# Weight sums by adding transfers and ScalarE copies instead of VectorE, and half of a group's first projection by 20 block products

## The chip, the cores and the metric

The kernel runs on one core of a Trainium2 chip, in float32. The metric is device time in microseconds of one launch, the median of several runs. Everything below concerns that one core: its TensorE (PE), VectorE (DVE), ScalarE (ACT), GpSimd (POOL), the SyncE queue (SP) that begins most loads, and the DMA engines.

## The reference

A gated linear attention is followed by a two-layer projection with SiLU between. Cut to what matters:

```
for t in range(768):                       # 4 batches x 8 heads, head size 48
    state = alpha[t][:, None] * state + outer(k[t], v[t])
    y[t]  = q[t] @ state
x = y as (3072 tokens, 384)
h = x @ w_in            # 384 x 2048
g = h * sigmoid(h)
out = g @ w_out         # 2048 x 384
```

The weights come as 64-bit floats and are rounded to float32 on the chip.

## The kernel before, in words

**Chunks and steps.** The 3072 tokens are cut into 24 chunks of 128 tokens (`n` = 0 to 23; `n` = 4 x position + batch). One step of the main loop works on two neighbouring chunks: `scores(n)` (PE products of `kp` and `qp`, copied by ACT into the tile `decayed`, then masked by POOL, line 813), `values(n)` (PE, copied by ACT into `xt`, line 851), `states(n)`, and for the next chunk `products` and `quotient` (all DVE: transposes at line 696, scans at 722 and 752, multiplications at 737, 739 and 758). A step has four slots. After each slot `fill` issues pieces of the projection until their share of work is due, so the PE always has projection work between the attention's short pieces. From the moment the tiles of `late` exist (`settle`, after the weights are converted, during chunk 7), every PE instruction is kept in the program's order, and so are the DVE sums.

**Groups.** Four chunks make a group (`grp` 0 to 5; 512 tokens), in two halves `h` of 256 tokens. The 2048 columns of `w_in` are taken as two pairs (`pair` 0 and 1). `enter_plain(grp, h, pair)` computes h = x @ w_in for one half and one pair the direct way: four pieces of six matmuls with 256 columns each, then one SiLU on ACT (line 909). `enter(grp, pair)` does both halves of a pair at once by a fast matrix multiplication on blocks: 20 products (list `PRODUCTS`) instead of the 24 of the direct way, a product being two matmuls. For this it needs sums of blocks of x (`sums_x`, list `SUMS_X`, 11 DVE instructions for each group) and sums of blocks of `w_in` (`sums_w`, list `SUMS_W`, 23 for each pair, once in the kernel). Blocks 0 to 11 are in the tile `w_in`, and are overwritten; 12 to 19 are in the tile `wx`. Then come copies and additions of the 20 results: ACT copies (line 936) and 14 DVE instructions (line 944, and 587 through `combine`) for each pair, and four SiLUs of double width (line 941). Three PSUM banks turn in this.

**Output.** `leave(grp, h)` computes out = g @ w_out by a scheme of seven products of eight matmuls; each product is a piece. `subtract` (line 1033) and `side_by_side` (line 1019) are DVE sums of parts of g that it needs. The results go out by transfers that POOL begins (line 1045).

**Order around the change.** Groups 0 and 1 are computed by `enter_plain`, groups 2 to 5 by `enter`. The list `pieces` has: all of group 0's plain pieces; `enter_plain(1, 0, 0)`; `leave(0, 0)`; `enter_plain(1, 1, 0)`; then the seven pieces of `leave(0, 1)` alternating with the eight of `enter_plain(1, 0, 1)` and `enter_plain(1, 1, 1)`; then for group 2 and the later ones `sums_x(grp)`, and `leave(grp-1, 0)` alternating with `enter(grp, 0)`, `leave(grp-1, 1)` with `enter(grp, 1)`. The sums of `w_in` are issued four at a time at the end of each `leave` piece (`done`): those of pair 0 during `leave(0, 1)`, those of pair 1 during `leave(1, 0)`.

The kernel also audits its inputs with DVE reductions (line 685), which start later, and has a general path that these inputs do not take.

Of the kernel before, what the change touches and what calls it, by code (L numbers as in the profile page):

```python
# [13 lines left out]
ALU = mybir.AluOpType  # L14
# [337 lines left out]
)  # L352


@with_exitstack
def quotients(
    ctx: ExitStack,
# [19 lines left out]
    dve, act, gps = nc.vector, nc.scalar, nc.gpsimd  # L377
# [197 lines left out]
    def block_w(at):  # L575

        return quads[:, at // NKT, at % NKT] if at < 4 * NKT else late["wx"][:, at - 4 * NKT]


    def combine(to, sa, a, sb, b):  # L580
        if sa == sb == 1:
            return dve.tensor_tensor(to, a, b, ALU.add)
        if sa == 1:
            return dve.tensor_tensor(to, a, b, ALU.subtract)
        if sb == 1:
            return dve.tensor_tensor(to, b, a, ALU.subtract)  # L586
        return dve.scalar_tensor_tensor(to, a, -1.0, b, ALU.mult, ALU.subtract)

    def sums_w(pair, upto):

        r = slice(2 * pair, 2 * pair + 2)
        while sums_done[pair] < min(upto, len(SUMS_W)):
            to, sa, a, sb, b = SUMS_W[sums_done[pair]]
            tc.keep_in_program_order(
                combine(block_w(to)[:, r], sa, block_w(a)[:, r], sb, block_w(b)[:, r]))
            sums_done[pair] += 1

    sums_done = [0] * (NQ // 2)
# [298 lines left out]
    def enter_plain(grp, h, pair):  # L897

        if h == 0:
            g_tiles(grp, pair)  # L900
        xt = xts[2 * grp + h]
        for f in range(8 * pair, 8 * pair + 8, 2):
            ps = bank(f // 2 % 3).rearrange("p (e n) -> p e n", e=2)
            for e in range(2):
                for t in range(NKT):
                    pe.matmul(ps[:, e, :], lhsT=w_in[:, t, (f + e) * 128 : (f + e + 1) * 128],
                              rhs=xt[:, t, :], start=(t == 0), stop=(t == NKT - 1))
            q, i = divmod(f, 4)
            act.activation(gts[grp, h, pair][:, i : i + 2, q % 2, :], ps, AF.Silu)  # L909
            if grp == 1 and pair == h == 0:  # L910
                differences(f // 2)
                differences(4 + f // 2)
            if grp > 0 and f % 8 == 6:
                side_by_side(grp, h, pair)
            yield

    def enter(grp, pair):
        g_tiles(grp, pair)
        halves = [gts[grp, h, pair] for h in range(2)]

        s = [halves[o % 2][:, o // 2] for o in range(8)]
        todo = iter(PRODUCTS)

        def new(i):
            return bank(i).rearrange("p (e n) -> p e n", e=2)

        def add(ps, first=False):
            w, x = next(todo)
            for e in range(2):
                pe.matmul(ps[:, e], lhsT=block_w(w)[:, 2 * pair + e], rhs=block_x(grp, x),  # L930
                          start=(first and e == 0), stop=(e == 1), skip_group_check=True)

        def copy(ps, to=None):
            if to is None:
                to = late["part"].tile([128, 2, TB], F32, name="part")
            act.copy(to, ps)  # L936
            return to

        def silu(h, i):
            x = halves[h][:, i : i + 2]  # L940
            act.activation(x, x, AF.Silu)  # L941

        def tt(to, a, b, op=ALU.add):
            dve.tensor_tensor(to, a, b, op)  # L944

        a, b, c = [new(i) for i in range(3)]
        add(a, True)
        copy(a, s[6])
        add(b, True)
        copy(b, s[2])  # L950
        add(c, True)
        tt(s[6], s[6], copy(c), ALU.subtract)
        yield
        add(a)
        t = copy(a)
        add(b)
        copy(b, s[4])
        add(c)
        copy(c, s[7])
        tt(s[7], s[7], t, ALU.subtract)  # L960
        yield
        add(a)
        copy(a, s[5])
        add(b)
        copy(b, s[3])
        tt(s[5], s[5], s[3])
        add(c)
        copy(c, s[0])
        yield
        add(a)  # L970
        tt(s[4], a, s[4])
        b = new(1)
        add(b, True)
        add(b)
        copy(b, s[1])
        yield
        c = new(2)
        add(c, True)
        tt(s[2], s[2], copy(c), ALU.subtract)
        a = new(0)  # L980
        add(a, True)
        tt(s[6], a, s[6])
        silu(0, 2)
        add(b)
        tt(s[5], copy(b), s[5], ALU.subtract)
        yield
        add(c)
        tt(s[1], c, s[1])
        tt(s[3], s[1], s[3], ALU.subtract)
        a = new(0)  # L990
        add(a, True)
        tt(s[2], a, s[2])
        add(b)
        tt(s[7], b, s[7])
        silu(1, 2)
        yield
        add(c)
        combine(s[1], -1, s[1], -1, s[0])
        tt(s[0], c, s[0])
        silu(0, 0)  # L1000
        a = new(0)
        add(a, True)
        tt(s[3], a, s[3])
        silu(1, 0)
        turn.append(turn.pop(0))
        for h in range(2):
            side_by_side(grp, h, pair)
        yield
# [7 lines left out]
    def side_by_side(grp, h, pair):  # L1016

        x = cells(grp, h, pair, 1, 0)
        dve.tensor_tensor(x, x, cells(grp, h, pair, 1, 1), ALU.add)

    def leave(grp, h):


        def product(ps, m, k, w, first=False):
            for i in range(HF):
                q = i // 2
                x = gts[grp, h, q // 2][:, 2 * (i % 2) + k, q % 2, m * C : (m + 1) * C]
                pe.matmul(ps, lhsT=x, rhs=w[:, i], start=(first and i == 0), stop=(i == HF - 1),
                          skip_group_check=True)

        def subtract(to, x, y):
            for pair in range(NQ // 2):
                dve.tensor_tensor(cells(grp, h, pair, *to), cells(grp, h, pair, *x),  # L1033
                                  cells(grp, h, pair, *y), ALU.subtract)

        def store(m, c, x, y=None):
            ci, b = divmod(GB * grp + 2 * h + m, B)
            o = opool.tile([128, HO], F32, name="o")
            if y is None:
                act.copy(o, x)  # L1040
            else:
                dve.tensor_tensor(o, x, y, ALU.add)  # L1042
            r = b * S + ci * C

            (gps if grp < NG - 1 else nc.sync).dma_start(out[r : r + C, c * HO : (c + 1) * HO], o)  # L1045

        u1, u2, u3, u4 = [rpool.tile([128, HO], F32, name=f"u{j}") for j in range(4)]
        steps = iter(range(7))

        def done():  # L1050
            if 2 * grp + h in (1, 2):
                sums_w(2 * grp + h - 1, 4 * next(steps) + 4)

        def new(i):
            return out_bank(i, HO)

        a, b = new(0), new(1)
        product(a, 0, 0, b11, True)
        act.copy(u1, a)
        subtract((0, 0), (1, 0), (0, 0))  # L1060
        done()
        yield
        product(b, 1, 0, t1, True)
        act.copy(u4, b)  # L1064
        done()
        yield
        product(a, 0, 1, b21)
        store(0, 0, a)
        subtract((0, 1), (0, 1), (0, 0))
        done()  # L1070
        yield
        b = new(1)
        product(b, 0, 0, t2, True)
        dve.tensor_tensor(u2, b, u1, ALU.add)
        subtract((1, 0), (1, 1), (0, 0))
        dve.tensor_tensor(u2, u2, u4, ALU.add)
        done()
        yield
        a = new(0)
        product(a, 0, 1, b22, True)  # L1080
        store(0, 1, a, u2)
        done()
        yield
        product(b, 1, 0, b12)
        dve.tensor_tensor(u3, b, u1, ALU.add)
        store(1, 1, u3, u4)
        done()
        yield
        a = new(0)
        product(a, 1, 1, t4, True)  # L1090
        store(1, 0, a, u3)
        done()
        yield
# [13 lines left out]
    def plain(grp, h, pair):  # L1107
        return (enter_plain(grp, h, pair), 12, 2 * (2 * grp + h) + 2)

    def group(grp):  # L1110
        return [[(enter(grp, pair), 12, GB * grp + GB)] * 7 for pair in range(2)]

    def output(grp):
        return [[(leave(grp, h), 12, GB * grp + GB)] * 7 for h in range(2)]
# [9 lines left out]
    pieces += [plain(1, 0, 0)] * 4 + [(leave(0, 0), 12, GB)] * 7  # L1124
    phases = [len(pieces)]
    pieces += [plain(1, 1, 0)] * 4
    both([(leave(0, 1), 12, GB)] * 7, [plain(1, 0, 1)] * 4 + [plain(1, 1, 1)] * 4)
    phases.append(len(pieces))
    before = output(1)
    for grp in range(2, NG):  # L1130
# [10 lines left out]
    def go_on():  # L1141

        nonlocal done
        next(pieces[done][0], None)
        done += 1

    audits = audit()
    done, bridged = 0, 0
    STEPS = NT + 1
    SLOTS = 4  # L1150
# [148 lines left out]
```

## Time and profile before

| | |
|---|---|
| median of 3 runs | 561.39 us (560.58 to 561.42) |
| span of the profiled execution | 558.1 us; the page gives no other time for it, so 3.3 us of the median lie around the span |
| PE busy | 541.4 us, 97% of the span |
| DVE busy | 445.1 us, 80% |
| ACT busy | 208.4 us, 37% |
| POOL busy | 75.9 us, 14% |
| granted TensorE clock | 0.994 on average |
| 46 sums of `w_in` on DVE | about 0.42 us each, between 150.7 us and 229 us |

A row of a timeline gives the start of a group of like instructions in us from the start of the span, the time to the end of its last one, the engine, the source line, the operation with output and inputs, the number of instructions (one float32 matmul of the program is two records on the PE), and, in brackets, how long the engine had been idle before and what released it. Matmuls are pipelined, so the distance between the starts of two neighbouring PE rows is what the first one costs.

### The profile page before, as it was taken

How to read it: one execution, taken by the hardware profiler on the slowest of the kernel's cores; microseconds unless marked ns; L12 is line 12 of the kernel's file. 1: busy time of each engine (PE TensorE's matmuls, PEld its weight loads, DVE VectorE, ACT ScalarE, POOL GpSimd, SP SyncE). 2: the span in 40 equal slices, each digit the busy share in tenths (PEclk: the TensorE clock that was granted, in tenths of full speed). 3: DMA queues.
4: the chain of work that ended last, by engine and by line, in shares of the span. 5: the costliest groups of instructions: out<-in, count | busy, mean ns of one | idle time of the engine just before them, and what ended most of it. 6: DMA issues, size and time to landing. Idle time of an engine off the chain costs nothing. (4 is left out here: it accounts for less than half of the span.)

```text
span 558.1 us, 12640 instructions
## 1 busy us (share of the span) xinstructions
PE 541.4 (97%) x5026; PEld 488.8 (88%) x5026; DVE 445.1 (80%) x801; ACT 208.4 (37%) x466; POOL 75.9 (14%) x146
## 2 busy tenths in 40 slices
PE   5999999999999999999999999999999999999996
PEld 3788887998899898899999999988998999998996
DVE  5887889974999799997998986998894775857531
ACT  3456643223333243353353353353263341432200
POOL 4100010221211211021021021021121000001000
PEclk9799999999999999999999999999999999999999
DMA  9999861164445525355445654717712122333101
GB/s 218 255 276 177 232 189 40 38 164 108 126 131 136 142 62 134 88 145 157 129 109 142 194 141 115 198 22 179 180 48 84 53 99 95 111 109 106 38 25 32
DMA packets 99220, 70.13 MB, mean 126 GB/s; under 512 B 56272, under 2 KB 88656, under 8 KB 99152
## 3 DMA queue, kind: packets, MB, share of 16 engines
q1 hardware_dynamic: 97232, 65.30, 44.6%
q0 software_dynamic: 1920, 3.93, 2.0%
q8 instruction: 41, 0.67, 0.5%
q14 instruction: 27, 0.22, 0.1%
HBM read 61.34 MB, written 7.86 MB: 124 GB/s over the span
## 5 line engine op out<-in xcount | busy, mean ns | idle before, releaser
L388 PE MATMUL ps_o<-w_out,g 128*128 128x192 f32 x768 | 134.7, 329 | 1.1 <-DVE o L1042 0.9
L388 PEld LDWEIGHTS ps_o<-w_out,g 128*128 128x128 f32 x768 | 125.4, 190 | 5.1 <-DVE o L1042 2.3
L388 PE MATMUL ps_m<-xt,w_in 128*128 128x256 f32 x480 | 113.6, 383 | 1.5 <-ACT xt L851 1.1
L388 PEld LDWEIGHTS ps_m<-xt,w_in 128*128 128x128 f32 x480 | 89.1, 190 | 14.4 <-ACT xt L851 1.6
L388 PE MATMUL ps_o<-wt,g 128*128 128x192 f32 x576 | 99.7, 326 | 0.0
L388 PEld LDWEIGHTS ps_o<-wt,g 128*128 128x128 f32 x576 | 95.1, 190 | 1.6 <-issue 0.2
L388 PE MATMUL ps_m<-xc,w_in 128*128 128x256 f32 x288 | 70.7, 382 | 0.0
L685 DVE TENSOR_REDUCE seen<-bits 128x1 f32<-128x384 int32 (+2 forms) x65 | 42.5, 689 | 24.0 <-DMA bits<-in_moe_w_out_dram 19.6
L388 PEld LDWEIGHTS ps_m<-xc,w_in 128*128 128x128 f32 x288 | 53.6, 190 | 7.0 <-DVE g L944 0.3
L941 ACT ACTIVATE g<-g 128x1024 f32<-128x1024 f32 x32 | 33.0, 1056 | 59.0 <-DVE g L944 59.0
L1033 DVE TENSOR_TENSOR g<-g 128x512 f32<-128x512 f32 x72 | 49.8, 708 | 6.1 <-PE ps_o L388 6.1
L1045 POOL DMA_DIRECT2D out_dram<-o x40 | 22.0, 550 | 223.2 <-DVE o L1042 127.6
L813 POOL TENSOR_SCALAR_AFFINE_SELECT g<-g 64x256 f32<-64x256 f32 x64 | 34.2, 534 | 124.8 <-ACT g L806 105.8
L388 PE MATMUL ps_m<-xc,wx 128*128 128x256 f32 x192 | 50.0, 383 | 1.0 <-DVE xc L586 1.0
L936 ACT COPY g<-ps_m 128x512 f32<-128x512 f32 x64 | 36.5, 588 | 36.5 <-PE ps_m L388 36.4
L388 PEld LDWEIGHTS ps_m<-xc,wx 128*128 128x128 f32 x192 | 35.2, 190 | 5.3 <-ACT u L1064 1.3
L944 DVE TENSOR_TENSOR g<-ps_m,g 128x512 f32<-128x512 f32 x56 | 37.0, 684 | 2.9 <-PE ps_m L388 2.7
L722 DVE TENSOR_TENSOR_SCAN u<-al,one 128x516 f32<-128x516 f32 x24 | 30.0, 1249 | 10.6 <-ACT al L719 10.3
L909 ACT ACTIVATE g<-ps_m 128x512 f32<-128x512 f32 x32 | 19.1, 596 | 42.8 <-PE ps_m L388 42.3
L936 ACT COPY part<-ps_m 128x512 f32<-128x512 f32 x32 | 18.9, 589 | 43.0 <-DVE g L944 21.3
L752 DVE TENSOR_TENSOR_SCAN p<-al,inv 128x516 f32<-128x516 f32 x24 | 29.9, 1246 | 1.0 <-PE ps_a L388 0.4
L388 PE MATMUL ps_a<-g,vn 128*32 128x128 f32 x768 | 27.5, 278 | 1.8 <-POOL g L801 1.7
(126 smaller groups left out, 611.4 us busy)
## 6 DMA issues: line engine op xcount, KB each, us to landing
bits<-in_moe_w_in_dram SPq DMA_DIRECT2D x24, 512.0 KB, 4.8
bits<-in_moe_w_out_dram SPq DMA_DIRECT2D x32, 384.0 KB, 3.1
at<-in_alpha_dram SPq DMA_DIRECT2D x64, 96.0 KB, 2.5
kt<-in_k_dram SPq DMA_DIRECT2D x64, 96.0 KB, 2.5
qt<-in_q_dram SPq DMA_DIRECT2D x64, 96.0 KB, 2.6
bits<-in_alpha_dram SPq DMA_DIRECT2D x9, 512.0 KB, 3.8
out_dram<-o POOLq DMA_DIRECT2D x40, 96.0 KB, 2.4
flips<-turn SPq DMA_DIRECT2D x12, 256.0 KB, 2.4
```

Source lines behind the costliest of these rows:

```text
L388: in_order(nc.tensor.matmul(*args, **kw))
L685: dve.tensor_reduce(seen[kind][which][:, i : i + 1], x, axis=AX, op=op, apply_absolute_value=True))
L722: dve.tensor_tensor_scan(u[:, end - 1 :: -1], sg[:, end:0:-1], one[:, end:0:-1], 0.0, ALU.mult, ALU.add)
L752: dve.tensor_tensor_scan(p[:, 0:end], sg[:, 0:end], iv[:, 0:end], 0.0, ALU.mult, ALU.add)
L813: gps.affine_select(x, x, pattern=[[0, NP], [1, CH]], compare_op=ALU.is_ge, fill=0.0, base=0, channel_multiplier=-1)
L909: act.activation(gts[grp, h, pair][:, i : i + 2, q % 2, :], ps, AF.Silu)
L936: act.copy(to, ps)
L941: act.activation(x, x, AF.Silu)
L944: dve.tensor_tensor(to, a, b, op)
L1033: dve.tensor_tensor(cells(grp, h, pair, *to), cells(grp, h, pair, *x), cells(grp, h, pair, *y), ALU.subtract)
L1045: (gps if grp < NG - 1 else nc.sync).dma_start(out[r : r + C, c * HO : (c + 1) * HO], o)
```

## The change

The 46 sums of `w_in` leave the DVE. Each is taken apart into operations of two kinds: a copy with a sign on ACT (`act.mul(to, a, +1 or -1)`), and a transfer from SBUF to SBUF begun by POOL that adds its source to its destination (`accum_op=ALU.add`). `sums_by_dma` makes a plan of 30 turns with at most one operation of each kind in a turn, an operation standing at least three turns after a transfer that it depends on: 22 copies and 23 transfers for each pair. The turns of pair 1 are issued first: three at the end of each piece of `leave(0, 0)` once `late` exists, and four after each piece of `enter_plain(1, 1, 0)`, so that the second pair of group 1 can be computed by `enter(1, 1)` in place of the eight plain pieces. Those of pair 0 are issued two at a time in `leave(0, 1)` and three at a time in `leave(1, 0)`. What is still due of a pair is issued when `enter` for that pair begins. `sums_x(1)` is added. In group 2 pair 1 is computed ahead of pair 0. The `side_by_side` of `enter_plain`'s groups is issued one piece later than before.

```diff
+def sums_by_dma(takes=3):
+    todo = []
+    for to, sa, a, sb, b in SUMS_W:
+        if to == a or (to != b and sa == -1):
+            sa, a, sb, b = sb, b, sa, a
+        first = sb if sa == 1 else -sb
+        if to != b or first == -1:
+            todo.append((to, b, first))
+        todo.append((to, a, 0))
+        if sa == -1:
+            todo.append((to, to, -1))
...
+    turns, free, read = [], {}, {}
+    while todo:
+        now, turn, held = len(turns), [], set()
+        kinds = set()
+        for op in list(todo):
+            to, a, sign = op
+            kind = bool(sign)
+            if (kind not in kinds and not {to, a} & held and (to not in held)
+                    and max(free.get(to, 0), free.get(a, 0), read.get(to, 0)) <= now):
+                turn.append(op)
+                todo.remove(op)
+                kinds.add(kind)
+                free[to] = now + (1 if sign else takes)
+                if a != to:
+                    read[a] = max(read.get(a, 0), free[to])
+            held |= {to, a}
+        turns.append(turn)
+    return turns
...
+    plan = sums_by_dma()
+
     def sums_w(pair, upto):
 
         r = slice(2 * pair, 2 * pair + 2)
-        while sums_done[pair] < min(upto, len(SUMS_W)):
-            to, sa, a, sb, b = SUMS_W[sums_done[pair]]
-            tc.keep_in_program_order(
-                combine(block_w(to)[:, r], sa, block_w(a)[:, r], sb, block_w(b)[:, r]))
+        while sums_done[pair] < min(upto, len(plan)):
+            for to, a, sign in plan[sums_done[pair]]:
+                to, a = block_w(to)[:, r], block_w(a)[:, r]
+                tc.keep_in_program_order(
+                    act.mul(to, a, float(sign)) if sign else
+                    gps.dma_start(to, a, accum_op=ALU.add))
             sums_done[pair] += 1
...
+            if grp == h == 1:
+                sums_w(1, sums_done[1] + 4)
             if grp > 0 and f % 8 == 6:
-                side_by_side(grp, h, pair)
+                owed.append((done, grp, h, pair))
             yield
 
     def enter(grp, pair):
+        sums_w(pair, len(plan))
         g_tiles(grp, pair)
...
-        steps = iter(range(7))
 
         def done():
-            if 2 * grp + h in (1, 2):
-                sums_w(2 * grp + h - 1, 4 * next(steps) + 4)
+            if grp == h == 0 and late:
+                sums_w(1, sums_done[1] + 3)
+            if (grp, h) in ((0, 1), (1, 0)):
+                sums_w(0, sums_done[0] + 2 + grp)
...
+    def second(grp, pair):
+        return [(enter(grp, pair), 12, GB * grp + GB)] * 7
+
     def group(grp):
-        return [[(enter(grp, pair), 12, GB * grp + GB)] * 7 for pair in range(2)]
+        return [second(grp, pair) for pair in ((1, 0) if grp == 2 else (0, 1))]
...
     pieces += [plain(1, 1, 0)] * 4
-    both([(leave(0, 1), 12, GB)] * 7, [plain(1, 0, 1)] * 4 + [plain(1, 1, 1)] * 4)
+    pieces.append((sums_x(1), 0, 2 * GB))
+    both([(leave(0, 1), 12, GB)] * 7, second(1, 1))
...
         next(pieces[done][0], None)
+        while owed and owed[0][0] < done:
+            side_by_side(*owed.pop(0)[1:])
         done += 1
```

More of the change, by code (lines that the diff above doesn't have):

```diff
@@ L352 @@
 )
+def sums_by_dma(takes=3):
[9 more added lines that the diff above has]
+            todo.append((to, to, -1))
+    for i in range(len(todo) - 1, 0, -1):
+        if todo[i] == todo[i - 1] and todo[i][2]:
+            del todo[i - 1 : i + 1]
+    turns, free, read = [], {}, {}
[16 more added lines that the diff above has]
+    return turns
 @with_exitstack
@@ L1144, in go_on @@
         next(pieces[done][0], None)
+        while owed and owed[0][0] < done:
+            side_by_side(*owed.pop(0)[1:])
         done += 1
     audits = audit()
+    owed = []
     done, bridged = 0, 0
```

## The prediction

> **What bounds the kernel now.** I read the page's busy line first, then the PE's timeline around the changed stage, then who the PE waited for, then the timelines of ACT, POOL and DVE there.
>
> ```profile
> PE 541.4 (97%) x5026; PEld 488.8 (88%) x5026; DVE 445.1 (80%) x801; ACT 208.4 (37%) x466; POOL 75.9 (14%) x146
> ...
> out_dram<-o POOLq DMA_DIRECT2D x40, 96.0 KB, 2.4
> ```
>
> PE is the bound, its 16.7 us of idleness lying mostly at the start and the end. So a matmul removed counts in full, unless the PE then waits. The PE's rows give prices:
>
> ```profile
> 150.00 2.75 PE L388 MATMUL ps_m<-xt,w_in 128*128 128x256 f32 x12
> 152.59 2.76 PE L388 MATMUL ps_o<-w_out,g 128*128 128x192 f32 x16
> ...
> 195.16 1.03 PE L388 MATMUL ps_m<-xc,wx 128*128 128x256 f32 x4
> 196.02 2.76 PE L388 MATMUL ps_o<-wt,g 128*128 128x192 f32 x16
> ```
>
> From start to start: a plain piece of six matmuls 2.59 us, a block product of two 0.86. Who the PE waited for:
>
> ```profile
> PE ps_m L388 <- DVE g L944: 1.3, 2, 0.9
> ...
> PE ps_a L388 <- DVE p L758: 0.5, 1, 0.5
> ```
>
> The 1.3 us lie at 219 and 230 us, where DVE has pair 1's sums between its other work; the 0.5 us is before chunk 9's scores at 143.87. The neighbours of the changed stage (ACT, then POOL, then DVE):
>
> ```profile
> 115.05 1.18 ACT L824 ACTIVATE st<-st,least 128x96 f32<-128x96 f32 x4
> 126.40 0.48 ACT L851 COPY xt<-ps_a 128x384 f32<-128x384 f32 x1 [10.17 <-PE ps_a L388]
> ...
> 130.72 0.65 ACT L806 COPY g<-ps_a 128x256 f32<-128x256 f32 x2 [0.30 <-PE ps_a L388]
> ...
> 138.62 0.60 ACT L909 ACTIVATE g<-ps_m 128x512 f32<-128x512 f32 x1 [1.99 <-PE ps_m L388]
> ```
>
> ```profile
> 120.37 0.56 POOL L1045 DMA_DIRECT2D out_dram<-o  x1 [4.88 <-DVE o L1042]
> 123.15 0.54 POOL L1045 DMA_DIRECT2D out_dram<-o  x1 [2.22 <-DVE o L1042]
> ...
> 131.44 1.83 POOL L813 TENSOR_SCALAR_AFFINE_SELECT g<-g 64x256 f32<-64x256 f32 x4 [4.83 <-ACT g L806]
> ```
>
> ```profile
> 139.25 0.69 DVE L1019 TENSOR_TENSOR g<-g 128x512 f32<-128x512 f32 x1 [7.62 <-ACT g L909]
> ...
> 143.03 0.69 DVE L758 TENSOR_TENSOR p<-turn,p 128x512 f32<-128x512 f32 x1
> ...
> 158.55 0.69 DVE L758 TENSOR_TENSOR p<-turn,p 128x512 f32<-128x512 f32 x1
> ```
>
> ACT and POOL are nearly idle from 116 to 126 us, but two of their results are due at once: the `xt` copy of chunk 7 at 126.40, which the plain piece at 126.93 reads, and the SiLU at 138.62. After that SiLU DVE runs `side_by_side`, the transposes, and p at 143.03 without a gap, and PE's scores wait for p. That chain has no slack.
>
> **What the Trainium skill says.** (1) "DMA: Bandwidth & Descriptors", anatomy of one DMA: a transfer begun by GpSimd takes about 2.0 us + bytes / 436e3, and any wait on a semaphore happens on the issuing sequencer before dispatch. For `out` (96 KB) that gives 2.23 us; the trace has 2.4 from issue to landing, so it agrees. The second half means that a transfer that waits holds up all of POOL's queue. (2) "Collectives: The Full Stack", the bandwidth ceiling: an add on the way reads two sources and emits two read descriptors for each chunk. No accumulating transfer is in this trace. (3) "ScalarE: Activation LUTs", what ACT_TABLE_LOAD costs: 186 ns + 0.833 ns per element with immediates, back-to-back overlap about 93. For 256 elements 399 ns; the trace has 376 for such a copy (line 806) and 0.65 us for two.
>
> **The change part by part.** The order of instructions in the two built programs shows that the change does what it says: 46 transfers, 44 ACT copies, 40 matmuls for 48.
>
> *PE.* 8 x 2.59 = 20.72 us of plain pieces become 20 x 0.863 = 17.26. **-3.46 us.** The reversed pairs of group 2 cost nothing: between the last product and `leave(2, 0)` stand chunk 15's values (2.24 us on PE), enough for the last addition and SiLU (0.69 + 1.06 us).
>
> *ACT.* 44 copies x 0.36 = 16 us, and in `enter(1, 1)` 12 copies (0.59) and 4 SiLUs (1.06) for 8 SiLUs (0.60): +6.5 us. ACT is 37% busy, so the work is covered; the waits are not.
>
> *Transfers of pair 1.* Two unknowns: I, POOL's time to issue one, and L, from the start of issue to landing. Bounds of I: below, 0.54 (`out`, 128 rows); above, 1.6, three times that, since a row here is two runs of 512 bytes and the add has a second read. I take 1.1. Bounds of L: below, 2.4; above, 4.5, about twice the page's 2.0 + 131072 / 436e3 = 2.30. I take 3.0. The program's order allows this walk:
> (a) ACT starts copies at 116.2. The second `out` of `leave(0, 0)` in this stretch is ready at 122.9 and goes (0.55) ahead of 15 += 9 and 16 += 5. The second lands at 123.5 + I + L. ACT's signed copy into block 5 waits for it, one more copy follows, and only then comes the `xt` copy of chunk 7 (0.5), in the same queue: PE goes on at 126.9 + d, with **d = I + L - 2.1** (2.0).
> (b) POOL's queue from 120.2: three `out` (1.65), two memsets (0.67) and eight transfers, then 10 += 12 starts at 122.5 + 8 I. It lands L later; ACT's sign of block 10, which waits, stands ahead of chunk 8's copies of scores; these and the four masks take to 3.1 us later; 10 += 1 is behind the masks and lands L later; ACT's next sign of block 10 waits for that ahead of the last two SiLUs (2.75 us with what lies between). So the SiLU of 138.62, which ended at 139.22, ends at 128.35 + 8 I + 2 L: **x = 8 I + 2 L - 10.9** late, or d if that is more. With 1.1 and 3.0: x = 3.9. All of it passes through DVE's chain to chunk 9's scores.
> Pair 0's plan is spread over two and three turns a `leave` piece, about 6 us with its neighbour, so its copies find their transfers landed: 0, up to 1 us if the POOL queue is late.
>
> *DVE.* From p(9) to p(10) before: 143.7 to 159.2, almost without a gap, 7 sums (3.05 us) among it. After: without those, with `sums_x(1)` (11 in 4.8 us, as group 2's at 190.4), two additions of `enter` (1.2) and one `subtract` more (0.6): 18.7 us by adding the distances between starts. PE's work between the two scores is 16.05 us (6 + 3 products, two `leave` pieces, values and scores). So PE waits 2.65 us at chunk 10's scores, whatever x is. To chunk 12 PE then has 28.7 us and DVE 27.5: PE leads again. Chunk 12's scores: 143.87 + x + 18.7 + 28.7 = 191.2 + x, against 192.49 before (-1.3 + x). Bounds of the DVE part: 0 lost if the sums of x find gaps, 3.5 if additions wait on ACT copies.
> From 197 to 229 us DVE is rid of pair 1's sums, and the 1.3 us of waits at 219 and 230 go: -1.3 (bounds -1.3 and 0).
> `side_by_side` one piece later: nothing; its reader is a `leave` 50 us on, and in the built order it still stands ahead of chunk 9's transposes.
>
> *Sum:* -3.46 + 2.65 - 0.5 (the old wait at 143.87, and rounding) + 3.9 - 1.3 = **+1.3 us**. The profiled execution spans 558.1, so about 559.4; with the 3.3 us that lie around it (median 561.39), 562.7.
>
> **Rivals.**
> *Cheap transfers (faster).* One mechanism, at one place: if 8 I + 2 L is under about 12.3, ACT and POOL keep up and x is only d. With I = 0.55, L = 2.4: d = 0.85, sum -1.7, 559.7 us. For it: `out`'s 0.54, and landing in SBUF instead of HBM. Against it: twice the runs and a second read.
> *POOL's issue becomes the bound of this stage.* With I = 1.6 and L = 3.0, x = 7.9; chunk 8's masks are late as well. Sum +5.3, 566.7 us. For it: eight transfers in series in (b) multiply each error of I by eight. Against it: the page's sentence that issue costs little.
> *Stalls cancel (no change).* Should x be 2 to 3.5, the products' gain and the waits meet within 1 us: 561.4. This needs I near 0.9.
> *DVE covers its share:* the sums of x run while DVE waits (it idles 7.6 us ahead of 139.25). Then -2.65, 560. Against it: DVE runs in order, and they stand behind p(9).
>
> **How the numbers follow.** About 0.2% (1.1 us) is what a measurement of this kernel can tell from no change. My forecast's case, slower by 1.2 to 4 us, has 0.39; POOL as the bound 0.18; no change 0.18; cheap transfers and covered sums 0.25 together. So faster 0.25, same 0.18, slower 0.57. The likeliest time is 562.8, the sum with a little for pair 0. The range goes from the cheap transfers, 559.2, to I = 1.6 with L = 3.5 (+6.3), 567.8; the forecast's own range is 562.5 to 565.5.
>
> **What would show it.** In the profile after: the time that POOL takes for a transfer of `wx` or `w_in` (0.9 to 1.3 us), and its landing (2.6 to 3.5); the `xt` copy of chunk 7 about 2 us after 126.4; ACT idle on transfers ahead of the signs of block 10; PE waiting on DVE p (line 758's successor) ahead of chunks 9 and 10's scores; no wait on DVE g near 219. The forecast is wrong if no PE wait over 1 us appears from 126 to 165 us, or if PE waits on transfers in pair 0's stretch (165 to 265), which I cost at nothing.

## The result and the profile after

The changed kernel takes **568.0 us** (median of 4 runs, 567.32 to 569.42), the kernel before, in the same comparison, 560.99 us (559.48 to 561.42). The ratio is 1.0131, 95% interval 1.0108 to 1.0154: it is **slower by 7.0 us**, five times what was forecast, and 0.2 us beyond the end of the range. The profiled execution spans 565.9 us against 558.1. In all runs with both figures, time and span lie 1.7 to 1.9 us apart. So the profiled execution before was one of about 559.8 us, faster than the median, and not one with 3.3 us around its span: a distance between the two traces is some 0.8 us larger than one between the medians.

From the page of the changed kernel, the busy line and the row of the granted TensorE clock in 40 slices:

```profile
PE 542.6 (96%) x5010; PEld 488.5 (86%) x5010; DVE 441.1 (78%) x780; ACT 228.4 (40%) x518; POOL 132.2 (23%) x192
...
PEclk9999999997999999999999999999999999999999
```

POOL's busy time has grown by 56 us, and in the tenth slice (127 to 141 us) the clock is not full. What PE waited for (us in total, times, longest), and the transfers (instructions, KB, median us from issue to landing):

```profile
PE ps_m L424 <- ACT xt L891: 5.2, 4, 4.3
...
PE ps_o L424 <- DVE o L1085: 2.0, 3, 1.3
PE ps_m L424 <- DVE inv L790: 1.9, 1, 1.9
```

```profile
wx<-w_in POOLq DMA_DIRECT2D x18, 128.0 KB, 5.0
w_in<-wx POOLq DMA_DIRECT2D x16, 128.0 KB, 4.4
...
w_in<-w_in POOLq DMA_DIRECT2D x12, 128.0 KB, 4.3
```

The 1.3 us on DVE g are gone. New is a wait of 4.3 us for `xt`. ACT's and then PE's timeline show it (start, time, what it is; in brackets the idle time before and its end), with PE's rows of the kernel before behind them:

```profile
129.16 0.42 ACT L634 ACTIVATE w_in<-w_in 128x256 f32<-128x256 f32 x1 [4.46 <-DMA wx<-w_in]
129.49 0.40 ACT L634 ACTIVATE w_in<-wx 128x256 f32<-128x256 f32 x1
129.79 0.46 ACT L891 COPY xt<-ps_a 128x384 f32<-128x384 f32 x1
...
144.98 0.58 ACT L949 ACTIVATE g<-ps_m 128x512 f32<-128x512 f32 x1
150.63 0.42 ACT L634 ACTIVATE w_in<-w_in 128x256 f32<-128x256 f32 x1 [5.07 <-DMA w_in<-wx]
150.96 0.46 ACT L891 COPY xt<-ps_a 128x384 f32<-128x384 f32 x1
```

```profile
130.31 5.49 PE L424 MATMUL ps_m<-xt,w_in 128*128 128x256 f32 x12 [4.34 <-ACT xt L891]
135.72 1.23 PE L424 MATMUL ps_a<-p,kp 48*64 48x128 f32 x32
...
151.47 0.89 PE L424 MATMUL ps_a<-p,kp 48*64 48x128 f32 x30 [0.84 <-ACT xt L891]
...
206.70 1.10 PE L424 MATMUL ps_m<-xc,wx 128*128 128x256 f32 x4 [1.93 <-DVE inv L790]
```

```profile
124.59 1.08 PE L388 MATMUL ps_a<-g,vn 128*32 128x128 f32 x32
...
126.93 2.86 PE L388 MATMUL ps_m<-xt,w_in 128*128 128x256 f32 x12 [0.26 <-ACT xt L851]
...
143.87 0.90 PE L388 MATMUL ps_a<-p,kp 48*64 48x128 f32 x32 [0.48 <-DVE p L758]
```

A sign by ACT waits 4.46 us for a transfer to land, the `xt` copy of chunk 7 stands behind it in ACT's queue, and PE stands idle. The plain piece that follows takes 5.49 us where it took 2.86 before. The windows view shows PE's clock there; after the busy times it gives 0.50:

```profile
130.30:135.70 5.40, 5.39 (x12) 3.87 (x12) 0.69 (x1) 0.00 (x0) 3.48 (x5) 0.50 1.17 200
```

At 150.63 the same happens again: a sign waits 5.07 us, and the `xt` copy of chunk 8 comes behind it, in the middle of chunk 9's scores.

**Where the time went.** The table gives for some kernels how late a chunk's scores start on PE against the kernel before, in us, and how late the last matmul ends. Both traces are counted from the start of chunk 7's values (124.59 us before, 123.88 after), which lie ahead of the difference.

| kernel | 8 | 9 | 10 | 12 | 13 | 14 | 16 | 23 | end |
|---|---|---|---|---|---|---|---|---|---|
| changed | 6.7 | 7.1 | 9.1 | 5.8 | 8.9 | 6.7 | 7.0 | 7.1 | 8.1 |
| busy_pe | 4.9 | 4.3 | 10.9 | 8.0 | 10.7 | 8.5 | 8.8 | 8.9 | 10.1 |
| few_early | 0.0 | 6.5 | 16.2 | 12.9 | 16.0 | 13.9 | 14.2 | 14.3 | 14.9 |
| plain_copy | 4.7 | 4.7 | 6.7 | 5.2 | 7.8 | 5.7 | 6.0 | 6.0 | 6.7 |
| no_wait | 0.0 | 0.3 | 2.3 | -0.9 | 1.7 | -0.5 | -0.2 | -0.2 | 1.7 |
| no_sums | 0.0 | 0.0 | 1.9 | -1.4 | 1.3 | -0.8 | -0.5 | -0.1 | 2.2 |
| no_sums_x | 0.0 | 0.0 | 0.0 | -3.2 | -0.5 | -2.6 | -2.3 | -2.4 | -0.8 |
| sums_dve | 0.0 | 0.7 | 2.5 | -0.8 | 1.3 | 1.5 | 1.8 | 1.8 | 3.0 |

(In the changed kernel, busy_pe and few_early chunk 9's scores stop behind the first two of 32 matmul records until `xt` is there; counted from the third they are 8.3, 8.4 and 7.6 late.) So in the changed kernel all is lost by chunk 9 or 10, 3.2 us come back up to chunk 12 with the products, 3 us are lost again ahead of chunk 13, 2.2 come back up to chunk 14, and about 1 us goes at the end.

### The profile page after: what moved, and what is told of

The parts are those of the page before. It is cut to its first block, busy times and chain, and to the rows that moved or that the text cites. A ratio compares the mean times of both kernels' runs of the same rounds, so it can differ in the third digit from the quotient of the medians.

```text
span 565.9 us, 12734 instructions
## 1 busy us (share of the span) xinstructions
PE 542.6 (96%) x5010; PEld 488.5 (86%) x5010; DVE 441.1 (78%) x780; ACT 228.4 (40%) x518; POOL 132.2 (23%) x192
## 3 DMA queue, kind: packets, MB, share of 16 engines
q0 software_dynamic: 14432, 9.97, 10.9%
## 5 line engine op out<-in xcount | busy, mean ns | idle before, releaser
L424 PE MATMUL ps_m<-xt,w_in 128*128 128x256 f32 x396 | 97.1, 390 | 5.2 <-ACT xt L891 5.2
L424 PEld LDWEIGHTS ps_m<-xt,w_in 128*128 128x128 f32 x396 | 75.2, 194 | 16.6 <-ACT xt L891 5.7
L424 PE MATMUL ps_m<-xc,w_in 128*128 128x256 f32 x324 | 79.6, 382 | 0.3 <-DVE xc L618 0.3
L424 PEld LDWEIGHTS ps_m<-xc,w_in 128*128 128x128 f32 x324 | 60.4, 190 | 7.9 <-DVE xc L618 0.4
L984 ACT ACTIVATE g<-g 128x1024 f32<-128x1024 f32 x36 | 37.4, 1056 | 61.5 <-DVE g L987 61.4
L424 PE MATMUL ps_m<-xc,wx 128*128 128x256 f32 x216 | 56.3, 383 | 3.0 <-DVE inv L790 1.9
L979 ACT COPY g<-ps_m 128x512 f32<-128x512 f32 x72 | 41.0, 588 | 40.6 <-PE ps_m L424 40.4
L987 DVE TENSOR_TENSOR g<-ps_m,g 128x512 f32<-128x512 f32 x63 | 41.7, 680 | 2.9 <-PE ps_m L424 2.6
L841 POOL TENSOR_SCALAR_AFFINE_SELECT g<-g 128x512 f32<-128x512 f32 x16 | 12.0, 771 | 83.8 <-ACT g L840 83.8
L424 PEld LDWEIGHTS ps_a<-p,kp 48*64 48x64 f32 (+1 forms) x640 | 21.5, 150 | 9.2 <-issue 5.2
```

Of the source, the lines that this page charges most:

```text
L424: in_order(nc.tensor.matmul(*args, **kw))
L841: gps.affine_select(g[:, u], g[:, u], pattern=[[0, NP], [1, C]], compare_op=ALU.is_ge, fill=0.0, base=0, channel_multiplier=-1)
```

## The experiments

Two theories stood against each other for the first stretch. **Chain of landings:** transfers and signs wait for one another, 30 turns long, and whatever stands behind a waiting sign in ACT's queue is late. **Load:** POOL's issue of 1.2 us each, the copies' work, or the traffic hold things back. For the second stretch: either DVE bounds the products, or the tail does. Each run gives its median and the ratio to the kernel before on the same chip.

| kernel | median us | ratio, 95% interval |
|---|---|---|
| busy_pe | 570.35 | 1.0184 (1.0152 to 1.0216) |
| few_early | 574.28 | 1.0242 (1.0222 to 1.0261) |
| signs_dve | 573.90 | 1.0226 (1.0201 to 1.0250) |
| plain_copy | 565.13 | one run; before 560.17 |
| no_wait | 562.17 | 1.0037 (1.0020 to 1.0053) |
| no_sums | 562.29 | 1.0039 (1.0026 to 1.0053) |
| no_sums_x | 560.36 | 0.9996 (0.9985 to 1.0008) |
| no_products | 576.34 | 1.0279 (1.0256 to 1.0302) |
| sbs_at_once | 567.37 | 1.0126 (1.0105 to 1.0147) |
| sums_dve | 563.74 | 1.0051 (1.0039 to 1.0064) |
| sums_pool | 574.70 | 1.0262 (1.0242 to 1.0283) |
| pool_before | 560.80 | 1.0012 (1.0002 to 1.0022) |
| no_audit_before | 558.42 | 0.9966 (0.9947 to 0.9985) |
| no_audit_after | 566.09 | 1.0105 (1.0074 to 1.0137) |
| no_audit_no_sums | 558.40 | 0.9954 (0.9937 to 0.9972) |
| audit_sooner | 589.63 | 1.0526 (1.0500 to 1.0552) |
| audit_spread | 578.31 | 1.0316 (1.0291 to 1.0341) |

### Is it the clock? (busy_pe)

```diff
                 if stage is values:
                     bridged = n + 1
+                if stage is states and n == 7:
+                    spin = bank(2, HO)
+                    for i in range(14):
+                        pe.matmul(spin, lhsT=wt[:, 0, 0, 0:128], rhs=wt[:, 1, 0, :],
+                                  start=(i == 0), stop=(i == 13), skip_group_check=True)
```

> The changed kernel with 14 more matmuls (128 x 192, into a bank that holds nothing then) behind the states of chunk 7, where PE stood idle for 4.34 us until the xt copy. The output is unaffected. First theory: the idleness itself halved PE's clock, so the plain piece took 5.49 us instead of about 2.87 and the scores 1.23 instead of 0.90, some 2.9 us. The added matmuls take 1.5 to 2 us out of the idle time; the granted clock should then stay at 1.00 from 130 to 137 us, the plain piece last about 2.8 us, and the time be 2 to 3 us under the changed kernel, about 565.5. Rival: the chain from the SiLU through DVE to chunk 9's scores is late anyway, by the transfers, and PE's slow piece only fills the waiting; then chunk 9's scores start as late as before, the clock shows 1.00 and the time stays within 0.5 us of 568.0.

A miss. PE's and ACT's timelines of this kernel:

```profile
130.94 2.86 PE L424 MATMUL ps_m<-xt,w_in 128*128 128x256 f32 x12 [0.38 <-ACT xt L891]
...
151.42 1.55 PE L424 MATMUL ps_a<-p,kp 48*64 48x128 f32 x30 [3.66 <-ACT xt L891]
152.90 3.78 PE L424 MATMUL ps_m<-xc,w_in 128*128 128x256 f32 x8
```

```profile
145.02 0.58 ACT L949 ACTIVATE g<-ps_m 128x512 f32<-128x512 f32 x1
150.58 0.42 ACT L634 ACTIVATE w_in<-w_in 128x256 f32<-128x256 f32 x1 [4.97 <-DMA w_in<-wx]
```

The first half of the theory held: with PE kept busy the plain piece takes 2.86 us again, and chunk 8 comes 1.9 us earlier. But the sign that holds back chunk 8's `xt` copy starts at 150.58, as in the changed kernel (150.63). PE waits 3.66 us there instead, and now that stretch runs at half the clock (8 matmul records in 3.78 us, 1.99 before). The rival's mechanism was right: the half clock filled time that the transfers' chain took anyway. Its number was not: the half clock at the new place costs, and the kernel is 2 to 3 us slower than the changed one (10.1 against 8.1 late at the end), not within 0.5.

### Is it the place of the first signs? (few_early)

```diff
-                sums_w(1, sums_done[1] + 4)
+                sums_w(1, sums_done[1] + 5)
...
-                sums_w(1, sums_done[1] + 3)
+                sums_w(1, sums_done[1] + 1)
```

> The changed kernel with only one turn of pair 1's plan in each piece of leave(0, 0), not three, and five instead of four in each plain piece behind it: no transfer is on its way when the xt copy of chunk 7 comes to ACT. First theory (landing of 4.4 to 5 us keeps ACT's signed copy, and with it the xt copy, back): the xt copy starts near 126.5 us again, the 4.34 us wait and the half clock go, but the transfers that are left stand ahead of the last SiLU and of enter(1, 1), so that 3 to 6 us of the lateness comes back at chunks 9 and 10: 563 to 568 us. Rival (the number of transfers in POOL's queue sets the end, not their place): the lateness at chunk 10's scores stays 8 us or more and the time is 568 or above.

A miss as well, by more than 6 us. From ACT's timeline:

```profile
125.69 0.48 ACT L891 COPY xt<-ps_a 128x384 f32<-128x384 f32 x1 [8.71 <-PE ps_a L424]
...
143.44 0.42 ACT L634 ACTIVATE w_in<-w_in 128x256 f32<-128x256 f32 x1 [4.60 <-DMA w_in<-w_in]
...
168.44 0.42 ACT L634 ACTIVATE w_in<-w_in 128x256 f32<-128x256 f32 x1 [8.94 <-DMA w_in<-w_in]
```

The first `xt` copy is in time, and chunk 8 is 0.0 late. But the chain has started later and ends later: the last sign of pair 1 comes at 168.44, in the changed kernel at 156.44, and chunk 10 is 16.2 us late. So this one wait is not the cost. What counts is when the whole chain is through: other due instructions of ACT stand behind its signs until then, and `enter(1, 1)` reads its results.

### The transfers without the waits (no_wait), and no sums (no_sums)

```diff
-                to, a = block_w(to)[:, r], block_w(a)[:, r]
+                a = block_r(a)[:, r]
+                if sign:
+                    to = late["wx"][:, spares[1] % 8, 2:4]
+                else:
+                    to = late["wx"][:, spares[0] % 8, 0:2]
+                spares[0 if not sign else 1] += 1
...
-                pe.matmul(ps[:, e], lhsT=block_w(w)[:, 2 * pair + e], rhs=block_x(grp, x),
+                pe.matmul(ps[:, e], lhsT=block_r(w)[:, 2 * pair + e], rhs=block_x(grp, x),
```

> The changed kernel with all 46 transfers and 44 copies and signs issued where they are, but into spare places (the eight blocks of wx, in turn) and from the w_in that is not summed, so that no instruction waits for a landing; products read the w_in that is not summed. The output is not the reference's. It has POOL's issue, ACT's copies and the memory traffic of the change, without the dependences. First theory (the chain of landings is what costs, 30 turns of a transfer or a sign, each waiting for the one before): the xt copy of chunk 7 at about 126.5 us, chunk 9's scores within 1 us of 143.3, and the time within 1.5 us of the 562.3 us of the kernel without sums. Rival (POOL's issue of 1.2 us each, or the traffic, holds masks and ACT back): chunk 9 still 2 us or more late, 565 us or above.

```diff
             for to, a, sign in plan[sums_done[pair]]:
-                to, a = block_w(to)[:, r], block_w(a)[:, r]
-                tc.keep_in_program_order(
-                    act.mul(to, a, float(sign)) if sign else
-                    gps.dma_start(to, a, accum_op=ALU.add))
+                pass
```

> The changed kernel without any sums of w_in: no transfers, no copies or signs by ScalarE; the products of pair 1 read a wx that is set to zero once and a w_in that is not summed, so the output is not the reference's. What is left of the change: 20 products for 8 plain pieces, sums_x(1), enter's additions, the order of the pairs, side_by_side a piece later. First theory (the products' saving of 3.46 us is real, and DVE keeps part of it back at chunk 10's scores and at the first products of group 2): chunk 9's scores within 0.5 us of 143.2, chunk 10's 1.5 to 3 us late by a wait on DVE p, chunk 12's 2 to 3.5 us early, and 554 to 558 us at the end, since DVE is also rid of 46 additions. Rival (the products themselves, with sums_x and enter, hold the end back): 560 us or more.

PE's timeline of no_wait:

```profile
126.86 2.86 PE L424 MATMUL ps_m<-xt,w_in 128*128 128x256 f32 x12 [0.26 <-ACT xt L901]
...
162.32 0.90 PE L424 MATMUL ps_a<-p,kp 48*64 48x128 f32 x32 [1.93 <-DVE p L808]
```

562.17 and 562.29 us: the same, as the first theory for no_wait had it. All 46 transfers are issued and land no sooner (median 5.1 us), all 44 copies are made, and it costs 0.3 us at chunk 9. So the load is not it. By the ratios, **waiting for landings makes 0.9 of the 1.3%, some 5 us**; the other 0.4%, about 2 us, is there without any sum and belongs to the products and what came with them. The first theory for no_sums was too hopeful by more than 4 us, and the rival's 560 us or more was met: chunk 9 is in time, chunk 10 is 1.9 us late by DVE p, as expected, but chunk 12 only 1.4 us early.

### How much of the landing is the add (plain_copy)

```diff
-                    gps.dma_start(to, a, accum_op=ALU.add))
+                    gps.dma_start(to, a))
```

> The changed kernel with its 46 transfers as plain copies between the same places, without the add; the output is not the reference's. It measures what of issue (1.18 us) and landing (median 4.6 us) is the add's. First theory[...]: issue stays near 1.1, landing 3 to 4 us, and the time 564 to 568 us. Rival (the add with its second read is the greater part): landing about 2.4 to 2.8 us, as the 96 KB out transfer has, and 561 to 564 us.

The group of POOL's issues (busy us, mean ns of one, idle before), and the landing of the transfers of `wx`:

```profile
L635 POOL DMA_DIRECT2D wx<-w_in x18 | 12.9, 716 | 7.3 <-ACT wx L634 5.9 <-DMA w_in<-wx 1.2 <-issue 0.2
```

```profile
DMA to landing us min/median/max: 2.2/3.3/5.4
```

With the add a transfer of `wx` takes 1.18 us to issue at the shortest (medians 1.22 and 1.53 for the two directions) and lands in 3.4 to 8.0 us, median 4.6; without it 0.72 and 3.3. Landing lies in the first theory's span, issue is quicker than it said. The lateness at chunk 9 goes with the landing: 0.3 us without waits, 4.7 with copies (one run), 7.1 to 8.3 with adds.

### Other queues and other ways for the sums (signs_dve, sums_dve, sums_pool, no_products)

```diff
-                    act.mul(to, a, float(sign)) if sign else
+                    dve.tensor_single_scalar(to, a, float(sign), ALU.mult) if sign else
```

> The changed kernel with the 44 copies and signs on DVE in place of ScalarE; the transfers as changed. DVE then waits for landings, and ACT never does. First theory (what costs is the queue that a due instruction shares with a sign that waits for a landing, not ACT as such): the xt copies of chunks 7 and 8 wait for nothing but PE, but DVE idles on transfers by 4 us and more at a time ahead of p(8) and p(9), and PE waits on DVE p: 566 to 580 us. Rival (ACT's own work is the trouble, and DVE with its free 7.6 us ahead of chunk 9 has room for it): 559 to 564 us.

```profile
PE ps_a L424 <- POOL g L853: 5.0, 1, 5.0
...
PE ps_m L424 <- DVE xc L618: 4.0, 2, 3.8
```

The waits move with the signs: `xt` is in time, but DVE stops up to 4.8 us ahead of one sign, POOL's masks come late behind transfers that wait for the signs, and `sums_x(1)` too. As the first theory said, it is the queue.

sums_dve replaces the transfers by one DVE addition for each sum, at three to a piece of pair 1 and four to a piece of `leave(1, 0)`:

```diff
-    plan = sums_by_dma()
+    plan = SUMS_W
...
-                    act.mul(to, a, float(sign)) if sign else
-                    gps.dma_start(to, a, accum_op=ALU.add))
+            to, sa, a, sb, b = SUMS_W[sums_done[pair]]
+            tc.keep_in_program_order(
+                combine(block_w(to)[:, r], sa, block_w(a)[:, r], sb, block_w(b)[:, r]))
```

> The changed kernel with all sums of w_in by DVE additions (one each, as in the kernel before), pair 1's 3 to a piece where the transfers were, pair 0's 4 to a piece of leave(1, 0); products, the order of the pairs and side_by_side as changed. No transfer adds. First theory (the transfers and ACT's signs behind them make the lateness of 6 to 8 us up to chunk 9, and the products save 3.46): the xt copy of chunk 7 comes at 126.5, full clock; DVE has 18 more additions of 0.44 us ahead of chunk 9, and one side_by_side less hurried, so 1 to 3 us late at chunks 9 and 10 by DVE, and the time is 559 to 563 us. Rival (DVE's overload by the products, sums_x and enter of pair 1 is the greater part): PE waits for DVE p at chunks 9 and 10 by 5 us or more, and the time is 565 or above.

It is the best form with products and sums, 0.8% under the changed kernel, and still 0.5% above the kernel before: 0.7 us late at chunk 9, 2.5 at chunk 10, and at the end 0.7 us beyond the first theory's span.

sums_pool gives each sum to one GpSimd instruction (`gps.tensor_tensor`), with a sign by ACT for two of the sums.

> The changed kernel with each sum of w_in by one GpSimd addition or subtraction (and for two of them one sign by ScalarE) in place of transfers, pair 1's three to a piece. DVE keeps out of it, and nothing waits for a landing. First theory (landing is what the transfers cost): GpSimd takes 0.6 to 1.2 us for 128 x 256, so 23 of them, one behind the other, are done by 150 us; chunk 9 is on time, chunk 10 as late as without sums (1.8 us), 562 to 564 us. Rival (GpSimd's additions slow DVE beside them, or take 2 us and more): DVE rows of 128 x 512 longer than 0.75 us, chunk 9 late by 2 us or more, and 566 us or above.

Another miss, with the same picture, from ACT's timeline:

```profile
129.27 0.42 ACT L636 ACTIVATE wx<-wx 128x256 f32<-128x256 f32 x1 [13.69 <-POOL wx L634]
129.60 0.46 ACT L895 COPY xt<-ps_a 128x384 f32<-128x384 f32 x1
```

The additions take 0.73 to 1.16 us (means of their groups), as expected. But one sign by ACT waits 13.69 us for POOL, with the `xt` copy behind it. DVE is busy for 451.4 us, 10 more than in the changed kernel, and one multiplication for p (128 x 512) took 1.03 us in place of 0.69, so the rival has its part too; how much of the time is whose was not isolated.

no_products leaves group 1 plain, takes the pairs of group 2 in the old order and issues the plans at the places of the kernel before, five turns at the end of each `leave` piece.

```diff
+            if 2 * grp + h in (1, 2):
+                p = 2 * grp + h - 1
+                sums_w(p, sums_done[p] + 5)
...
-    both([(leave(0, 1), 12, GB)] * 7, second(1, 1))
+    both([(leave(0, 1), 12, GB)] * 7, [plain(1, 0, 1)] * 4 + [plain(1, 1, 1)] * 4)
```

> The transfers and ACT's signs without the products: group 1's pair 1 stays in plain pieces as before, pair 0's plan lies in the pieces of leave(0, 1) and pair 1's in those of leave(1, 0), five turns to a piece, both pairs of groups 2 on in the old order; side_by_side a piece later. 44 copies and 46 transfers remain, at places where their first reader is about 50 us off. First theory (transfers cost only where a due xt copy or SiLU stands behind a sign that waits for one): copies of ACT wait for landings here too, 5 turns to a piece of about 5.5 us, so some PE waits on xt of 1 to 3 us each appear; DVE is rid of 28 additions and its waits of 1.3 us go: 560 to 566 us. Rival (the add transfers slow everything that reads the same memory): PE and ACT rows beside them grow by over 5%, and the time is above 568.

576.34 us, above the first theory's span and in the rival's. PE's timeline has the waits:

```profile
173.66 4.93 PE L424 MATMUL ps_m<-xt,w_in 128*128 128x256 f32 x12 [5.26 <-ACT g L949]
...
227.48 1.55 PE L424 MATMUL ps_a<-p,kp 48*64 48x128 f32 x30 [6.13 <-ACT xt L891]
```

With the first reader of a pair's sums 50 us behind the pair's first transfer, signs that wait for landings still hold an SiLU and an `xt` copy back, PE stands for 5.3 and 6.1 us, and each time it comes back at a lower clock (4.93 us for a plain piece of 2.75, 1.55 for scores of 0.90). ACT's copies keep their 0.40 to 0.42 us, so the rival's reason, slower memory, is not seen: its number is met by the first theory's mechanism, with waits twice as long as expected.

### Where the products' saving went (no_sums_x, sbs_at_once, no_audit)

no_sums_x is no_sums with `xc` of group 1 set to zero by GpSimd in place of `sums_x(1)`'s additions.

> The kernel without sums of w_in, and also without the 11 sums of x for group 1 on DVE (its xc is set to zero by GpSimd); the output is not the reference's. First theory (with the products in place DVE is the bound from chunk 9 on, so PE's 3.46 us are given up to waits on DVE at chunk 10 and at the start of group 2): the wait of 1.76 us at chunk 10's scores goes, chunk 12's scores come 3 to 4.5 us ahead of 192.5, the wait of 1.56 us near 200 us shrinks below 0.5, and the time is 557.5 to 560 us. Rival (something else, such as the order of pairs or the tail's reads for the audit, sets the end): chunk 12 as without sums of w_in, or the end within 1 us of 562.3.

The wait at chunk 10 goes, and chunk 12 is 3.2 us early: there the products' 3.46 us are nearly whole. The time falls from 0.4% above the kernel before to level with it, so these 11 sums alone cost about 2.4 us. Then 2.7 us are lost up to chunk 13, exactly as in no_sums. The wait near 200 us did not shrink (1.6 us), and the median is 0.4 us above the first theory's span. DVE is the reason that the profile offers; the windows view from 184 to 207 us, of the kernel before and of no_sums (PE, PEld, DVE, ACT, POOL busy us with instructions, clock, DMA):

```profile
184.00:207.00 23.00, 23.00 (x226) 20.98 (x225) 20.16 (x40) 9.79 (x25) 2.94 (x5) 1.00 0.38 101
```

```profile
184.00:207.00 23.00, 21.01 (x214) 18.73 (x213) 22.44 (x42) 10.78 (x24) 4.25 (x8) 1.00 0.37 101
```

DVE is busy for 22.44 of 23 us with products, 20.16 without. `sums_x(2)` begins at 192.49 us, before it was 190.39, while PE arrives earlier. That this alone is the cause was not isolated. The order of the pairs in group 2, which is reversed in every kernel with products, is a rival that no run tried alone.

sbs_at_once takes back the third part of the change:

```diff
-                owed.append((done, grp, h, pair))
+                side_by_side(grp, h, pair)
```

> The changed kernel with side_by_side at once, as in the kernel before; all else as changed. First theory (putting it off leaves two of them, with p of chunk 12, ahead of sums_x(2), which makes part of the 2.2 us that PE waits for DVE at 199 and 207 us): these two waits shrink by 1 to 2 us, the stretch up to chunk 12 stays as late as before, and the time is 566 to 567.5 us. Rival (sums_x(2) is late by what DVE has to do anyway, or the saving is taken by the chain at chunk 9, where side_by_side would now stand ahead of the transposes): within 0.7 us of 568.0 or above.

567.37 us lies in the spans of both theories, and its interval overlaps that of the changed kernel. The waits decide: 0.3 and 1.8 us near 199 and 206 us, where there were 0.3 and 1.9. That part of the change does nothing measurable, and it is not what makes `sums_x(2)` late: the rival.

**The tail.** no_sums is 0.1 us early at chunk 23 and ends 2.2 us late. Its PE and DVE timelines there:

```profile
517.99 3.25 PE L424 MATMUL ps_o<-w_out,g 128*128 128x192 f32 x16 [1.25 <-DVE o L1083]
```

```profile
511.96 1.01 DVE L723 TENSOR_REDUCE seen<-bits 128x1 f32<-128x384 int32 x2 [1.00 <-DMA bits<-in_moe_w_out_dram]
...
516.07 1.00 DVE L723 TENSOR_REDUCE seen<-bits 128x1 f32<-128x384 int32 x2
...
517.59 0.35 DVE L1083 TENSOR_TENSOR o<-ps_o,u 128x192 f32<-128x192 f32 x1
```

From about 457 to 521 us the audit reads the second weights, a load and two reductions about every 4.1 us. DVE's `o` at 517.59, for which PE waits, stands behind a pair of reductions that waited 1.0 us for their load and behind the next pair. Three kernels leave the readings of both weights out:

```diff
-        if wide:
+        if False:
             todo += [(moe_w_in[t * 128 : t * 128 + 128, c : c + 512], 512, 1)
...
```

> The kernel before without its second reading of moe_w_in and moe_w_out and the 56 DVE reductions on them (all behind 300 us), so the check of these weights' sizes is left out; the output doesn't depend on it here. It is the base for the next two. First theory (in the last 70 us DVE's o stands behind reductions that wait for loads, one pair every 4.1 us): PE's waits on DVE o, 0.9 us in the kernel before, go, and the time is 558.5 to 560 us. Rival (the tail is PE's alone): 560.3.

> The changed kernel without any sums of w_in, and with the same readings left out; the output is not the reference's. First theory (the products are 0.5 us ahead at chunk 16's scores, and the tail's reductions turn that into 1.9 us behind): it ends within 1 us of the kernel before without the readings, likely 0.3 to 0.8 us ahead of it. Rival (the products cost that much elsewhere): 1.5 to 2.5 us behind it.

> The changed kernel with the same left out. First theory: PE's waits on DVE o, 2.0 us there, go, and it ends 6.0 to 6.6 us behind the kernel before without the readings, as chunk 16's scores do (6.3), in place of 7.6. Rival: 7.3 us or more behind.

Medians 558.42, 558.40 and 566.09 us. The kernel before gains 2.5 us by it, although in the traces its waits on DVE `o` only fall from 0.9 to 0.5 us. Without the readings no_sums is level with the kernel before, where with them it was 2.1 us behind: the first theory, though the hoped 0.3 to 0.8 us ahead are only in the traces (0.3), not in the medians. The changed kernel stays 7.7 us behind, the rival of its expectation; its lateness of 7 us at chunk 16 simply stays.

### A faster version? (pool_before, audit_sooner, audit_spread)

pool_before is the kernel before with its sums as GpSimd additions.

> The kernel before (no products in group 1, its places for the sums) with the 46 sums of w_in by GpSimd in place of DVE. First theory: the 1.3 us that PE waits for DVE g at 219 and 230 us goes, GpSimd is free enough, and the time is 559 to 560.5 us, 0.1 to 0.4% faster than before. Rival (masks and the queue of out transfers stand behind GpSimd's additions): PE waits for POOL g or ACT, 561 to 565 us.

560.80 us: no difference that counts (at most 0.2%). The waits on DVE g fall from 1.3 to 0.7 us, and those on DVE `o` grow from 0.9 to 3.0; counted as in the table, it is 0.9 us late at chunk 23 and 2.5 at the end.

The other two issue the audit's readings in each slot, or in three of four:

```diff
-        if at % 2 == 0 and step > 3 * GB + 2:
+        if step > 3 * GB + 2:
```

> The kernel before with the second reading of the weights begun in every slot from step 15 on in place of every other slot, so that none is left for the last 70 us; nothing else is changed. It asks whether the 2.5 us that the readings cost can be had without leaving them out. First theory: DVE has room for the reductions between 250 and 440 us (it is 92% busy there, and each takes 0.69 us), so the tail loses its waits and the time is 558.5 to 560 us. Rival: DVE is full there, new waits of PE on DVE g or p appear, and the time is 560.5 to 564 us.

> The same, begun at step 15 as before but in three slots of four. First theory: fewer reductions meet a busy DVE, a few are left for the tail, 559 to 560 us. Rival as for every slot: 560.5 to 563 us.

Both far worse than either theory had it. From DVE's timeline of audit_sooner:

```profile
287.61 1.22 DVE L685 TENSOR_REDUCE seen<-bits 128x1 f32<-128x1024 f32 x1 [3.67 <-DMA bits<-in_alpha_dram]
```

A reduction that waits for its load stands ahead of `sums_x` at the beginning of a group, and PE waits for `xc` 23.0 us in two waits. No version tried that does all of the kernel's work beats the kernel before.

## Why the prediction was wrong

The sign was right and the mechanism was the one named, a sign by ACT that waits for a landing ahead of a due copy; the sizes were off, and the sum's list was too short.

- **L, the landing, is the term that failed.** Taken as 3.0 us, with 4.5 as its upper bound; measured 4.6 as the median for `wx`, and up to 8.0. I, taken as 1.1, measured 1.18 at the shortest, with medians of 1.22 and 1.53. With I = 1.2 and L = 4.6 the prediction's own walk gives d = 1.2 + 4.6 - 2.1 = 3.7 and x = 9.6 + 9.2 - 10.9 = 7.9, and the sum +5.3 in place of +1.3. The trace has 4.1 for the `xt` copy and 7.1 for the end of the SiLU. For d this is a sound walk with a wrong input. For x the agreement is in part luck, since PE's piece at half clock, which the walk did not have, lies ahead of that SiLU too; but in busy_pe, where PE keeps its clock there, the signs hold the SiLU back to the same 145.0 us, 7.2 us late. The bound was about twice 2.30 us, an estimate for 128 KB by the fit in the Trainium skill's "DMA: Bandwidth & Descriptors" (anatomy of one DMA). Even without the add these transfers took 3.3 us. The range ended at 567.8 (561.39 and 6.3 are 567.7) because L went into it as 3.5 us, not as the bound of 4.5.
- **The walk ended too soon.** It followed x through DVE to chunk 9's scores. The next sign, at 150.63, waited 5.07 us more, ahead of chunk 8's `xt` copy, and that ended last (busy_pe).
- **The clock was not priced.** A wait of 2 us was forecast; at 4.34 us the clock fell to 0.50, which made 2.6 us of chunk 8's 6.7. The Trainium skill has this in "TensorE: Matmul & The Clock Gate" (Part 1: the HAM clock gate): half rate after about 3.4 us of idleness. In the changed kernel it lay beside the chain, and busy_pe shows no gain from removing it.
- **-3.46 us for the products** was right as a saving of PE: 32.42 us from chunk 10's to chunk 12's scores before, 29.20 after (-3.2, forecast -3.7).
- **+2.65 at chunk 10** was right in kind: from chunk 9 to 10, 1.9 are lost in no_sums and 1.8 in sums_dve. In the changed kernel PE was late already, and 0.8 to 2 us show between chunks 9 and 10.
- **-1.3 from 219 to 230 us** came: the waits are gone, and 2.2 us come back between chunks 13 and 14. But 2.1 to 3.1 us that the sum did not have were lost just ahead, at the start of group 2, in every kernel of the table, all of which have the products. For no waits at all the sum gave -2.6; at chunk 16 it was -0.5 (no_sums).
- **The tail** was nowhere in the sum, and by the traces took 1.0 us in the changed kernel and 2.3 in no_sums. The medians without the readings confirm it for no_sums, not for the changed kernel.
- **Pair 0 at 0** was nearly right: against no_wait the changed kernel is 6.7 us late at chunk 10 and 7.2 at chunk 13, so pair 0's chain costs about 0.4 us. **`side_by_side` at 0** was right.
- Of the rivals, "POOL's issue becomes the bound" came nearest with 566.7 us, and for the wrong reason: in no_wait POOL issues as many transfers, and chunk 9 is 0.3 us late. "Cheap transfers" fell with L.

## What to carry to other kernels

A transfer that another engine's queue waits for can cost its whole landing, here 3.4 to 8.0 us, once for each link of a chain of them, and the bill is paid by whatever stands behind the waiting instruction: count the links, and measure the landing of that kind of transfer in a small run before a plan relies on it. Relief for the busiest engine counts only up to the next engine's floor. Here DVE was 98% busy in the stretch behind the saving, and the tail ran at the pace of its loads; the products' 3.46 us were given back, so look at both before counting a saving.

## What was not expected of the hardware

- A transfer of 128 KB from SBUF to SBUF lands in 3.3 us (median of those on `wx`), with an add in 4.6; POOL's issue is 0.72 us, and with the add 1.18 at the shortest. The Trainium skill's "Collectives: The Full Stack" (the bandwidth ceiling) has an add read two sources; this agrees in direction with 1.6 times the issue.
- PE's clock fell to 0.54 after a gap of only 2.02 us (sbs_at_once, ahead of chunk 9's scores, which took 1.51 us for 0.90), while one of 1.76 us in no_sums and one of 2.33 us in signs_dve (also ahead of chunk 9's scores) left it at 1.00. So the length of the gap alone does not decide it here. The 2.02 us are shorter than the 3.4 us of the skill's page on the clock gate, and the measurement decides.
